# The last two pairs of token tiles: one after the other instead of side by side

## The chip, the cores and the metric

One core of a Trainium2 chip. The time is device microseconds of one execution of the whole program; less is better. The core's engines run side by side and wait for one another through semaphores: TensorE (PE, matmuls; PEld is its weight load) writes to PSUM, VectorE (DVE) and ScalarE (ACT) read PSUM and write SBUF, GpSimd (POOL) works on SBUF, and SyncE (SP) issues most of the transfers.

## The reference

Attention within clusters on 4 batches of 8 heads, 768 positions, 64 dimensions; its output, as 3072 tokens of 512, goes through a gated feed-forward layer:

```python
x = np.ascontiguousarray(attn_out.transpose(0, 2, 1, 3)).reshape(B * S, H * D)
gate = 1.0 / (1.0 + np.exp(-(x @ w_gate)))    # 512 x 1536
val = x @ w_val                               # 512 x 1536
return (gate * val @ w_out).astype(np.float32)  # w_out: 1536 x 512
```

Only the end of the feed-forward layer is touched here.

## The kernel before

**Stages.** The batches go one after the other. Attention of a batch writes transposed tokens `xT`; the feed-forward work of a batch is cut into two blocks of 384 tokens (three tiles of 128), put into a list `queue` of small pieces ("atoms") and taken from there between attention steps by `ffn_run`, which has a budget in ns. When all attention is done, the last block (batch 3, block 1, tiles 3 to 5) is queued with `final=True` and runs to the end with nothing else beside it but `aside` (below).

**Gate and value groups** (`ffn_atoms`). For each of the 12 slices `fc` of the 1536 hidden values, a gate atom does four matmuls of 384 columns into a bank of the PSUM `ring` (L529) and a tanh on ScalarE (L535); a value atom does four more into the next ring bank (L545), and VectorE joins both into slice `fc` of `hT` (L550). The ring has four banks handed out in turn; a bank is written again only when its last reader is done.

**Output products** (`product_out`). From batch 1 on, `hT @ w_out` is done for pairs of token tiles (t1, t2) in a scheme with seven products instead of eight. With the hidden dimension cut into two halves of 6 slices, and the 512 output columns into two of 256, the left side is a 2x2 matrix of blocks (row: t1 or t2; column: hidden half), and so is `w_out` (B11, B12, B21, B22; T1 to T4 are sums of them made once). The sums of the left side are made by VectorE (`Sums.make`, L626 to L632): 1 = both halves of t2, 2 = sum 1 - t1's first half, 3 = t1's first half - t2's first half, 4 = t1's second half - sum 2, written over sum 2. A product of one pair is six matmuls of 256 columns (L713), in this order:

| product | left | adds into | what follows |
|---|---|---|---|
| 1 | t1, first half | x, fresh | ScalarE copies x to C11 |
| 4 | t2, second half | y, fresh | C21 = y + C11 |
| 6 | sum 2 | x, fresh | C12 = x + C11 |
| 5 | sum 1 | y, fresh | C22 = y + C11, then sum 4 |
| 7 | sum 3 | x, on top of 6 | C21 += x, C22 += x, store row t2 |
| 3 | sum 4 | y, on top of 5 | C12 += y |
| 2 | t1, second half | x (last block: a ring bank) | C11 += it, store row t1 |

The additions are `plus` (L658), the copy L662. `x` and `y` are the two banks of the PSUM pool `op`, taken through `out_bank`, which hands the two out in turn. `begin` decides which of them is x:

```python
slot = taken["op"] % 2
u = [out_bank() for _ in range(2)]
x = 0 if slot != taken["last"] else 1
taken["last"] = (slot + x) % 2
```

In block 0 of a batch there is one pair, (0,1): its 14 atoms (half products of three matmuls) go to the list `aside`, and `ffn_run` then takes an atom from `aside` and one from `queue` by turns. In batch 3 they so alternate with the first 14 gate and value atoms of the last block. In block 1 there are two pairs, (3,2) and (4,5) (tile 2 was left over from block 0). They run **side by side**: each product is done for both pairs, in the two halves of one bank, and an addition covers both (512 columns). In the last block the products start after all 12 gate and value groups. Product 2 is there done by `closing` (L727): (3,2) whole, (4,5) in two halves of 128 columns, each into a ring bank of its own, each with its addition and its store.

When the sums are made is in a table: after value group `fc`, these sums of these pairs.

```python
1: [(1, (3, 2))], 5: [(2, (3, 2)), (3, (3, 2))], 6: [(3, (4, 5))],
11: [(1, (4, 5)), (2, (4, 5))],
```

**Stores** (`store`, L502). One transfer on SP's queue for each; in batch 3 it is issued as soon as SP reaches it and its data is ready. SP works strictly in order. Output tiles `ob` are `[128, 2, 512]` floats: row 0 is t1's, row 1 t2's (side by side: one tile for both t1, one for both t2).

Of the kernel before, what the change touches and what calls it, by code (L numbers as in the profile page):

```python
# [8 lines left out]
FP = mybir.dt.float32  # L9
HP = mybir.dt.float16  # L10
# [88 lines left out]
def kernel(  # L99
# [397 lines left out]
    def tok(b, t, f):  # L497
        return HB[b, t // 3][:, HF * f : HF * f + HF, bass.ts(t % 3, 128)]
# [16 lines left out]
    def ffn_atoms(xT, t0, n, b, final=False):  # L515
        blk = t0 // 384
        gv = []
        cost = NDC * max(n, 80) / 2.4 + 3
        pairs = [] if b < PB else [(0, 1)] if blk == 0 else [(3, 2), (4, 5)]
        sm = {x: Sums(b, *x) for x in pairs}  # L520

        def gate(fc, st):
            def f():
                need(("w", fc // WQ, 0), *(("x", b, p, t0 // 128 + c) for p in range(NP) for c in range(n // 128)))
                if fc == 0:
                    HB[b, blk] = htp.tile([128, NFC, 384], HP, name="hT")
                g = bank(512, name="g")
                for dc in range(NDC):
                    PE.matmul(  # L529
                        out=g[:, 0:n], lhsT=wg[fc // WQ][:, dc, fc % WQ, :],  # L530
                        rhs=xT[:, dc, t0 : t0 + n],
                        start=(dc == 0), stop=(dc == NDC - 1),
                    )
                th = thp.tile([128, 384], FP, name="th")
                ACT.activation(th[:, 0:n], g[:, 0:n], AF.Tanh)  # L535
                st.append(th)

            return f

        def val(fc, st):  # L540
            def f():
                need(("w", fc // WQ, 1))
                w = bank(512, name="v")
                for dc in range(NDC):
                    PE.matmul(  # L545
                        out=w[:, 0:n], lhsT=wv[fc // WQ][:, dc, fc % WQ, :],
                        rhs=xT[:, dc, t0 : t0 + n],
                        start=(dc == 0), stop=(dc == NDC - 1),
                    )
                DVE.scalar_tensor_tensor(  # L550
                    HB[b, blk][:, fc, 0:n], st[0][:, 0:n], 1.0, w[:, 0:n], ALU.add, ALU.mult
                )
                for k, x in SUMS_AT[b >= PB, blk].get(fc, []):
                    sm[x].make(k)
                if fc == NFC - 1 and pairs and blk == 0:
                    aside.extend(product_out(b, [sm[(0, 1)]], False))

            return f

        for fc in range(NFC):  # L560
            st = []
            gv.append((cost, gate(fc, st)))
            gv.append((cost, val(fc, st)))
        outs = []
        if b < PB:
            for t in range(n // 128):
                outs += plain_out(b, blk, t)
        elif blk == 1:
            outs = product_out(b, [sm[x] for x in pairs], final)
        return gv + outs  # L570

    def plain_out(b, blk, t):
        OA = SCHED.get(f"oa{b}{384 * blk}", SCHED.get("oa", 4))
# [33 lines left out]
        },  # L607
    }

    class Sums:  # L610


        def __init__(self, b, t1, t2):
            self.b, self.t1, self.t2, self.of = b, t1, t2, {}

        def make(self, i):
            a1 = lambda f: tok(self.b, self.t1, f)
            a2 = lambda f: tok(self.b, self.t2, f)
            if i == 4:
                self.of[4] = self.of[2]  # L620
            else:
                t = sump.tile([128, HF, 128], HP, tag="sum", name="sum")
                self.of[i] = t
            o = self.of[i]
            if i == 1:
                DVE.tensor_tensor(o, a2(0), a2(1), ALU.add)  # L626
            elif i == 2:
                DVE.tensor_tensor(o, self.of[1], a1(0), ALU.subtract)
            elif i == 3:
                DVE.tensor_tensor(o, a1(0), a2(0), ALU.subtract)  # L630
            else:
                DVE.tensor_tensor(o, a1(1), o, ALU.subtract)  # L632

    def product_out(b, sums, final):


        P_ = len(sums)
        st = {}

        def begin():  # L640
            need(*(("wo", i) for i in range(WOP)), *(("wt", i, c) for i in range(4) for c in range(2)))
# [4 lines that stand above are left out]
            taken["pair"] = True  # L646
            for z, t in (("x", u[x]), ("y", u[1 - x])):
                st[z] = t[:, 0 : P_ * HD].rearrange("p (e m) -> p e m", m=HD)
            if P_ == 1:
                ob = osp.tile([128, 2, DM], FP, name="ob")  # L650
                st["o1"], st["o2"] = ob[:, 0:1], ob[:, 1:2]
            else:
                st["o1"] = osp.tile([128, 2, DM], FP, name="ob")
                st["o2"] = osp.tile([128, 2, DM], FP, name="ob")
            for o in ("o1", "o2"):
                st[o, 0], st[o, 1] = st[o][:, :, 0:HD], st[o][:, :, HD:DM]

        plus = lambda dst, a, z: DVE.tensor_tensor(dst, a, z, ALU.add)  # L658
        C11, C12, C21, C22 = ("o1", 0), ("o1", 1), ("o2", 0), ("o2", 1)

        def end1():
            ACT.activation(st[C11], st["x"], AF.Copy)  # L662

        def end4():
            plus(st[C21], st["y"], st[C11])

        def end6():
            plus(st[C12], st["x"], st[C11])

        def end5():  # L670
            plus(st[C22], st["y"], st[C11])
            for m in sums:
                m.make(4)

        def end7():
            plus(st[C21], st["x"], st[C21])
            plus(st[C22], st["x"], st[C22])
            for i, m in enumerate(sums):
                store(st["o2"][:, i], b, m.t2, 1)

        def end3():
            plus(st[C12], st["y"], st[C12])
            if final:
                store(st[C12], b, sums[0].t1, P_, slice(HD, DM))

        def end2():
            plus(st[C11], st["x"], st[C11])
            taken["pair"] = False
            store(st["o1"], b, sums[0].t1, P_)

        steps = [
            ("x", lambda m: tok(b, m.t1, 0), B11, True, end1),
            ("y", lambda m: tok(b, m.t2, 1), T4, True, end4),
            ("x", lambda m: m.of[2], T2, True, end6),
            ("y", lambda m: m.of[1], T1, True, end5),
            ("x", lambda m: m.of[3], T3, False, end7),
            ("y", lambda m: m.of[4], B22, False, end3),
            ("x", lambda m: tok(b, m.t1, 1), B21, True, end2),
        ]
        atoms = []  # L700
        G = SCHED.get("og", 3)

        def atom(k, e, g):
            z, lhs, rhs, start, end = steps[k]

            def f():
                if k + e + g == 0:
                    while aside and P_ > 1:
                        aside.pop(0)[1]()
                    begin()  # L710
                a = lhs(sums[e])
                for c in range(g, g + G):
                    PE.matmul(  # L713
                        out=st[z][:, e], lhsT=a[:, c, :], rhs=rhs[:, c, :],
                        start=start and c + e == 0, stop=c == HF - 1, skip_group_check=True,
                    )
                if g + G == HF and e == P_ - 1:
                    end()

            return f  # L720

        def closing(e, a, z):
            def f():
                o = bank(z - a, name="o_end")
                lhs = tok(b, sums[e].t1, 1)
                for c in range(HF):
                    PE.matmul(  # L727
                        out=o, lhsT=lhs[:, c, :], rhs=B21[:, c, a:z],
                        start=c == 0, stop=c == HF - 1,
                    )  # L730
                m = st["o1"][:, e, a:z]
                plus(m, o, m)
                store(m.unsqueeze(1), b, sums[e].t1, 1, slice(a, z))

            return f

        for k in range(6 if final else 7):
            for e in range(P_):
                for g in range(0, HF, G):
                    atoms.append((G * (HD / 2.4 + 2.5), atom(k, e, g)))  # L740
        if final:
            for e, a, z in ((0, 0, HD), (1, 0, HD // 2), (1, HD // 2, HD)):
                atoms.append((900, closing(e, a, z)))
        return atoms

    queue = []
# [754 lines left out]
```

## Time and profile before

| | us |
|---|---|
| three runs: median (lowest to highest) | 324.35 (324.08 to 324.59) |
| the profiled run | 324.13 |
| its span in the profile | 322.3 |
| busy in the span: TensorE, ScalarE, VectorE, GpSimd | 314.6, 231.3, 226.4, 108.6 |

The span runs from the first to the last recorded instruction; the run's own time is 1.8 us longer. In the profile's lines, a group is given as line, engine, operation, output<-inputs, shape and count; in a timeline, start and length come first. A matmul's recorded length reaches past the start of the next one: matmuls overlap, so their rate is read from starts. The clock is that granted to TensorE, 1.00 being full.

### The profile page before, as it was taken

To read this page: it belongs to the slowest core of one execution; us is meant where nothing else is said; L and a number is where in the kernel's file an instruction comes from. 1 tells how busy PE (TensorE), PEld (TensorE's weight loads), DVE (VectorE), ACT (ScalarE), POOL (GpSimd) and SP (SyncE) were. 2 spreads that over 40 slices of the span, in tenths; PEclk is the share of its full clock that TensorE was granted. 3 is DMA by queue.
4 is the path that set the end of the run, shared out by engine and by line. 5 is a ranking of instruction groups with operands and counts; after the bars stand their busy time and mean duration, and the time that the engine had idled before them with its cause. 6 is when DMAs were issued, how large, how long until landed. Compare 5 with 4: busy or idle time off the path is not lost.

```text
span 322.3 us, 9168 instructions
## 1 busy us (share of the span) xinstructions
PE 314.6 (98%) x3510; PEld 222.1 (69%) x3510; DVE 226.4 (70%) x588; ACT 231.3 (72%) x520; POOL 108.6 (34%) x145
## 2 busy tenths in 40 slices
PE   7999999999999999999999999999999999999995
PEld 5888666766766656666777687666777688566674
DVE  5899656777667997576879588676867356555655
ACT  6688988787898977877767866788777886332220
POOL 5887464154335275433143342523111111000000
PEclk9999999999999999999999999999999999999999
DMA  6999996738988677974694652952503112200103
GB/s 205 379 253 171 259 169 120 205 85 232 248 121 226 112 218 153 229 175 130 116 212 121 202 113 60 288 124 52 111 2 91 39 26 79 77 2 1 67 0 130
DMA packets 77835, 45.15 MB, mean 140 GB/s; under 512 B 56864, under 2 KB 75232, under 8 KB 77792
## 3 DMA queue, kind: packets, MB, share of 16 engines
q1 hardware_dynamic: 73824, 39.73, 48.2%
q0 software_dynamic: 3680, 4.72, 9.0%
q8 instruction: 27, 0.44, 0.6%
q14 instruction: 16, 0.13, 0.1%
q10 hardware_dynamic: 288, 0.13, 0.1%
HBM read 28.34 MB, written 6.29 MB: 107 GB/s over the span
## 4 chain that ended last, share of the span: by engine, by line
PE 91%; DVE 6%; issue 1%; ACT 1%; ACTq 0%; POOL 0%; DVEq 0%
PE g L529 19%; PE v L545 19%; PE sc L803 18%; PE o L713 12%; PE av L826 10%; PE o L583 4%; PE lg L434 2%; PE lg L421 1%; PE t_ps L1052 1%; PE oh_ps L1112 1%; DVE lgs L449 0%; DVE T L1065 0%; DVE vheld L276 0%; PE vs_ps L354 0%; PE o_end L727 0%
## 5 line engine op out<-in xcount | busy, mean ns | idle before, releaser
L808 ACT ACTIVATE es<-sc 128x384 f16<-128x384 f32 x384 | 174.7, 492 | 40.0 <-PE sc L803 30.7
L803 PE MATMUL sc<-T 128*128 128x384 f16 x384 | 117.8, 326 | 1.0 <-DVE lgs L449 0.6
L826 PEld LDWEIGHTS <-es 128*128 128x128 f16 x1152 | 81.4, 98 | 35.3 <-issue 0.2
L826 PE MATMUL av<-va,es 128*128 128x65 f16 x1152 | 97.6, 194 | 0.0
L550 DVE SCALAR_TENSOR_TENSOR hT<-th,v 128x384 f16<-128x384 f32 x96 | 53.1, 553 | 55.8 <-PE av L826 36.6
L529 PE MATMUL g<-xTb,wg 128*128 128x384 f16 x384 | 78.2, 326 | 0.1
L545 PE MATMUL v<-xTb,wv 128*128 128x384 f16 x384 | 78.1, 326 | 0.0
L535 ACT ACTIVATE th<-g 128x384 f32<-128x384 f32 x96 | 47.2, 492 | 32.8 <-PE g L529 13.7
L375 POOL TENSOR_TENSOR xp<-t,rec 128x384 f16<-128x384 f32 (+1 forms) x30 | 21.8, 728 | 100.4 <-DVE rec L372 49.9
L529 PEld LDWEIGHTS <-wg 128*128 128x128 f16 x384 | 37.2, 97 | 19.7 <-issue 0.4
L545 PEld LDWEIGHTS <-wv 128*128 128x128 f16 x384 | 37.4, 98 | 19.0
L803 PEld LDWEIGHTS <-T 128*128 128x128 f16 x384 | 37.1, 97 | 0.7 <-DVE T L1133 0.7
L1369 POOL TENSOR_TENSOR hl<-kraw,hl 128x384 f16<-128x384 f32 x22 | 20.2, 920 | 42.0 <-DVE hl L1368 19.6
L658 DVE TENSOR_TENSOR ob<-o,ob 128x256 f32<-128x256 f32 (+1 forms) x41 | 21.9, 547 | 8.8 <-PE o L713 8.1
L713 PEld LDWEIGHTS <-sum 128*128 128x128 f16 x216 | 20.9, 98 | 5.6 <-DVE sum L632 0.7
L1369 POOL TENSOR_TENSOR hl<-qraw,hl 128x384 f16<-128x384 f32 x22 | 20.7, 940 | 10.0 <-DVE hl L1368 9.7
L713 PE MATMUL o<-wo,hT 128*128 128x256 f16 x150 | 22.5, 272 | 0.0
L370 DVE TENSOR_TENSOR t<-av,sv 128x390 f32<-128x390 f32 (+1 forms) x30 | 14.4, 479 | 8.2 <-PE av L826 7.3
L583 PE MATMUL o<-wo,hT 128*128 128x512 f16 x72 | 19.9, 379 | 0.0
L713 PEld LDWEIGHTS <-hT 128*128 128x128 f16 x150 | 14.6, 97 | 3.7
L449 DVE TENSOR_REDUCE lgs<-lg 128x192 f32<-128x384 f32 x23 | 12.7, 550 | 2.8 <-PE lg L434 2.6
L322 POOL CAST va<-vraw 128x768 f16<-128x768 f32 x15 | 13.0, 868 | 2.6 <-DMA vraw<-in_v_dram 2.6
(143 smaller groups left out, 324.9 us busy)
## 6 DMA issues: line engine op xcount, KB each, us to landing
vraw<-in_v_dram SPq DMA_DIRECT2D x15, 384.0 KB, 4.8
kraw<-in_k_dram SPq DMA_DIRECT2D x14, 384.0 KB, 4.0
out_dram<-ob SPq DMA_DIRECT2D x19, 256.0 KB, 2.3
qraw<-in_q_dram SPq DMA_DIRECT2D x12, 384.0 KB, 4.3
wg<-in_moe_w_gate_dram POOLq DMA_DIRECT2D x2, 768.0 KB, 9.6
wv<-in_moe_w_val_dram POOLq DMA_DIRECT2D x2, 768.0 KB, 10.6
wo<-in_moe_w_out_dram POOLq DMA_DIRECT2D x2, 768.0 KB, 9.3
T<-ohT SPq DMA_DIRECT2D x44, 24.0 KB, 1.9
```

Of the source, the lines that this page charges most:

```text
L375: (eng or POOL).tensor_tensor(x, t[:, 0:nq, 0:64], bcast(rec[:, 0:nq], 64), ALU.mult)
L529: PE.matmul(out=g[:, 0:n], lhsT=wg[fc // WQ][:, dc, fc % WQ, :], rhs=xT[:, dc, t0 : t0 + n], start=(dc == 0), stop=(dc == NDC - 1),)
L535: ACT.activation(th[:, 0:n], g[:, 0:n], AF.Tanh)
L545: PE.matmul(out=w[:, 0:n], lhsT=wv[fc // WQ][:, dc, fc % WQ, :], rhs=xT[:, dc, t0 : t0 + n], start=(dc == 0), stop=(dc == NDC - 1),)
L550: DVE.scalar_tensor_tensor(HB[b, blk][:, fc, 0:n], st[0][:, 0:n], 1.0, w[:, 0:n], ALU.add, ALU.mult)
L583: PE.matmul(out=o, lhsT=HB[b, blk][:, fc, bass.ts(t, 128)], rhs=wo[fc // WON][:, fc % WON, :], start=(fc == 0), stop=(fc == NFC - 1),)
L658: plus = lambda dst, a, z: DVE.tensor_tensor(dst, a, z, ALU.add)
L713: PE.matmul(out=st[z][:, e], lhsT=a[:, c, :], rhs=rhs[:, c, :], start=start and c + e == 0, stop=c == HF - 1, skip_group_check=True,)
L803: PE.matmul(out=sc.rearrange("p (c t) -> p c t", t=128), lhsT=s["k"], rhs=s["q"], start=True, stop=True,)
L808: ACT.activation(es, sc, AF.Exp, scale=SCALE)
L826: PE.matmul(out=av[:, a0 + s["c0"] + i, :], lhsT=s["es"][:, bass.ts(i, 128)], rhs=VA[b, p][:, e, s["j"], :], start=(first and i == 0 and a ...
L1369: POOL.tensor_tensor(hl[:, :, 64:128], r, hl[:, :, 0:64], ALU.subtract)
```

## The change

`product_out` loses its `final` branch. The last block's pairs are done by a new function `closing`: the first four products (1, 4, 6, 5) of (3,2) are cut in halves of three matmuls, and one half goes behind each of the atoms from gate group 7 to value group 10; gate and value group 11 follow. Then, whole: 7 of (3,2); 1 and 4 of (4,5); 3 of (3,2); 6 and 5 of (4,5); 2 of (3,2); 7 and 3 of (4,5); 2 of (4,5) in two halves. Pair (3,2) has the two banks of `op`; pair (4,5) takes four ring banks for its x and y (1 and 4, then 6 and 5), and product 2 takes ring banks as before. An addition covers one pair (256 columns). Stores: after product 7 row t2 (256 KB), after 3 the right half of row t1 (128 KB), after 2 the left half (128 KB, for (4,5) one store after both halves). The sums that need the last slices are made in two parts, slices 0 to 4 of a half after value group 10 and slice 5 after group 11; sum 4 has a tile of its own.

```diff
+        when = SUMS_LAST if final else SUMS_AT[b >= PB, blk]
...
-                for k, x in SUMS_AT[b >= PB, blk].get(fc, []):
-                    sm[x].make(k)
+                for k, x, *c in when.get(fc, []):
+                    sm[x].make(k, *c)
...
-            outs = product_out(b, [sm[x] for x in pairs], final)
+            outs = product_out(b, [sm[x] for x in pairs])
+        if final:
+            return closing(b, gv, sm[(3, 2)], sm[(4, 5)])
         return gv + outs
+
+    def closing(b, gv, ma, mb):
...
+            rhs = {1: B11, 2: B21, 3: B22, 4: T4, 5: T1, 6: T2, 7: T3}
...
+            def product(k, g=0, n=HF):
+                def f():
+                    z = {1: "a", 4: "d", 6: "x", 7: "x", 5: "y", 3: "y"}[k]
+                    if g == 0 and k in (1, 4, 6, 5):
+                        if k == 1:
+                            st["ob"] = osp.tile([128, 2, DM], FP, name="ob")
+                        st[z] = bk(z)
+                    o = st[z][:, 0:HD]
+                    mm(o, k, g, n, k not in (7, 3))
+                    if g + n < HF:
+                        return
+                    if k == 1:
+                        ACT.activation(C(0, 0), o, AF.Copy)
+                    elif k == 4:
+                        plus(C(1, 0), o, C(0, 0))
+                    elif k == 6:
+                        plus(C(0, 1), o, C(0, 0))
+                    elif k == 5:
+                        plus(C(1, 1), o, C(0, 0))
+                    elif k == 7:
+                        plus(C(1, 0), o, C(1, 0))
+                        plus(C(1, 1), o, C(1, 1))
+                        store(st["ob"][:, 1:2], b, m.t2, 1)
+                    else:
+                        plus(C(0, 1), o, C(0, 1))
+                        store(st["ob"][:, 0:1, HD:DM], b, m.t1, 1, slice(HD, DM))
...
+            def last(parts):
+                def f():
+                    for a, z in parts:
+                        o = bank(z - a, name="o_end")
+                        mm(o, 2, 0, HF, True, a, z)
+                        plus(st["ob"][:, 0, a:z], o, st["ob"][:, 0, a:z])
+                    store(st["ob"][:, 0:1, 0:HD], b, m.t1, 1, slice(0, HD))
...
+        def bank_a(z):
+            if z in "ad":
+                need(*(("wo", i) for i in range(WOP)), *(("wt", i, c) for i in range(4) for c in range(2)))
+                two[z] = out_bank()
+            return two[{"x": "a", "y": "d"}.get(z, z)]
+
+        pa, la = pair(ma, bank_a)
+        pb, lb = pair(mb, lambda z: bank(512, name="o_end"))
+        early = [pa(k, g, HF // 2) for k in (1, 4, 6, 5) for g in (0, HF // 2)]
...
+        early[0] = drained(early[0])
+        atoms = gv[:14]
+        for i, x in enumerate(gv[14:]):
+            atoms.append(x)
+            if i < len(early):
+                atoms.append((0.0, early[i]))
+        for f in (
+            pa(7), pb(1), pb(4), pa(3), pb(6), pb(5), la([(0, HD)]), pb(7), pb(3),
+            lb([(0, HD // 2), (HD // 2, HD)]),
+        ):
+            atoms.append((0.0, f))
+        return atoms
...
+    SUMS_LAST = {
+        1: [(1, (3, 2))], 5: [(2, (3, 2)), (3, (3, 2))], 6: [(3, (4, 5))],
+        10: [(4, (3, 2), 0, 5), (1, (4, 5), 0, 5), (2, (4, 5), 0, 5), (4, (4, 5), 0, 5)],
+        11: [(4, (3, 2), 5, 6), (1, (4, 5), 5, 6), (2, (4, 5), 5, 6), (4, (4, 5), 5, 6)],
+    }
```

More of the change, by code (lines that the diff above doesn't have):

```diff
@@ L552, in f @@
                 )
-                for k, x in SUMS_AT[b >= PB, blk].get(fc, []):
-                    sm[x].make(k)
+                for k, x, *c in when.get(fc, []):
+                    sm[x].make(k, *c)
                 if fc == NFC - 1 and pairs and blk == 0:
-                    aside.extend(product_out(b, [sm[(0, 1)]], False))
+                    aside.extend(product_out(b, [sm[(0, 1)]]))
             return f
@@ L568, in ffn_atoms, with pair, mm, drained @@
         elif blk == 1:
-            outs = product_out(b, [sm[x] for x in pairs], final)
+            outs = product_out(b, [sm[x] for x in pairs])
+        if final:
+            return closing(b, gv, sm[(3, 2)], sm[(4, 5)])
         return gv + outs
+    def closing(b, gv, ma, mb):
+        ac, order = [], []
+        plus = lambda dst, a, z: DVE.tensor_tensor(dst, a, z, ALU.add)
+        def pair(m, bk):
+            st = {}
+            lhs = {
+                1: lambda: tok(b, m.t1, 0), 2: lambda: tok(b, m.t1, 1), 4: lambda: tok(b, m.t2, 1),
+                6: lambda: m.of[2], 5: lambda: m.of[1], 7: lambda: m.of[3], 3: lambda: m.of[4],
+            }
+            rhs = {1: B11, 2: B21, 3: B22, 4: T4, 5: T1, 6: T2, 7: T3}
+            C = lambda i, j: st["ob"][:, i, HD * j : HD * j + HD]
+            def mm(o, k, g, n, start, a=0, z=HD):
+                w = lhs[k]()
+                for c in range(g, g + n):
+                    PE.matmul(
+                        out=o, lhsT=w[:, c, :], rhs=rhs[k][:, c, a:z],
+                        start=start and c == 0, stop=c == HF - 1, skip_group_check=True,
+                    )
+            def product(k, g=0, n=HF):
[24 more added lines that the diff above has]
+                        store(st["ob"][:, 0:1, HD:DM], b, m.t1, 1, slice(HD, DM))
+                return f
+            def last(parts):
[5 more added lines that the diff above has]
+                    store(st["ob"][:, 0:1, 0:HD], b, m.t1, 1, slice(0, HD))
+                return f
+            return product, last
+        two = {}
+        def bank_a(z):
[6 more added lines that the diff above has]
+        early = [pa(k, g, HF // 2) for k in (1, 4, 6, 5) for g in (0, HF // 2)]
+        def drained(f):
+            def g():
+                while aside:
+                    aside.pop(0)[1]()
+                f()
+            return g
+        early[0] = drained(early[0])
[10 more added lines that the diff above has]
+        return atoms
@@ L608 @@
     }
+    SUMS_LAST = {
[3 rows of a table added]
+    }
     class Sums:
@@ L614, in __init__, with make @@
             self.b, self.t1, self.t2, self.of = b, t1, t2, {}
[L616 to L624, printed above, removed]
+        def make(self, i, c0=0, c1=HF):
+            c = slice(c0, c1)
+            a1 = lambda f: tok(self.b, self.t1, f)[:, c]
+            a2 = lambda f: tok(self.b, self.t2, f)[:, c]
+            if c0 == 0:
+                if i == 4 and c1 == HF:
+                    self.of[4] = self.of[2]
+                elif i == 4:
+                    self.of[4] = tp.tile([128, 12, 128], HP, tag="T", name="T")[:, 0:HF]
+                else:
+                    self.of[i] = sump.tile([128, HF, 128], HP, tag="sum", name="sum")
+            o = self.of[i][:, c]
             if i == 1:
@@ L627, in make @@
             elif i == 2:
-                DVE.tensor_tensor(o, self.of[1], a1(0), ALU.subtract)
+                DVE.tensor_tensor(o, self.of[1][:, c], a1(0), ALU.subtract)
             elif i == 3:
@@ L631, in make, with product_out @@
             else:
-                DVE.tensor_tensor(o, a1(1), o, ALU.subtract)
-    def product_out(b, sums, final):
+                DVE.tensor_tensor(o, a1(1), self.of[2][:, c], ALU.subtract)
+    def product_out(b, sums):
         P_ = len(sums)
@@ L682, in end3 @@
             plus(st[C12], st["y"], st[C12])
-            if final:
-                store(st[C12], b, sums[0].t1, P_, slice(HD, DM))
         def end2():
@@ L720, in atom @@
             return f
[L722 to L737, printed above, removed]
+        for k in range(7):
             for e in range(P_):
@@ L740, in product_out @@
                     atoms.append((G * (HD / 2.4 + 2.5), atom(k, e, g)))
-        if final:
-            for e, a, z in ((0, 0, HD), (1, 0, HD // 2), (1, HD // 2, HD)):
-                atoms.append((900, closing(e, a, z)))
         return atoms
```

## The prediction

> **What bounds the kernel now.** I read the page first: busy time, the clock, the chain that ended last.
>
> ```profile
> span 322.3 us, 9168 instructions
> PE 314.6 (98%) x3510; PEld 222.1 (69%) x3510; DVE 226.4 (70%) x588; ACT 231.3 (72%) x520; POOL 108.6 (34%) x145
> PEclk9999999999999999999999999999999999999999
> PE 91%; DVE 6%; issue 1%; ACT 1%; ACTq 0%; POOL 0%; DVEq 0%
> ```
>
> TensorE is busy 98% of the span at full granted clock, and the chain is 91% TensorE. The program's matmuls stay the same in number and shape, so the change can move time only in two ways: TensorE gaps after the point where the two programs part, and what follows the last matmul. That point is gate group 7 of the last block: both programs issue the same up to there. So next I read the chain in order of time, and the windows of the last 20 us.
>
> ```profile
> 302.23 0.33 PE o L713 x3
> 302.56 0.65 PE g L529 x4
> 309.06 7.98 PE o L713 x72
> 317.04 1.34 PE o_end L727 x18
> 318.38 0.02 issue
> 318.40 0.29 DVE ob L658
> 302.40:309.06 6.66, 6.66 (x44) 4.06 (x42) 3.52 (x7) 2.46 (x5) 0.00 (x0) 1.00 0.11 42
> 309.06:318.40 9.34, 9.30 (x91) 8.05 (x88) 7.07 (x13) 0.60 (x1) 0.00 (x0) 1.00 0.04 15
> 318.40:321.40 3.00, 0.00 (x0) 0.00 (x0) 0.29 (x1) 0.00 (x0) 0.00 (x0) 1.00 0.86 302
> ```
>
> (In the windows, after the length: busy us of PE, PEld, DVE, ACT, POOL, then clock, DMA share, GB/s.) The prices of TensorE are here: a group of four 384-column matmuls takes 0.65 us, three 256-column ones 0.33, so a product of one pair (six) 0.65; the 18 closing matmuls take 1.34, of which 6 are 256 wide (0.65), so each half of the last product costs 0.345. TensorE has no gap worth naming, and it ends at 318.40. The last 3.9 us are stores. Their issues, and the time to landing:
>
> ```profile
> 317.19 0.33 SPq L502 DMA_DIRECT2D out_dram<-ob  x1
> 317.57 0.42 SPq L502 DMA_DIRECT2D out_dram<-ob  x1
> 318.09 0.40 SPq L502 DMA_DIRECT2D out_dram<-ob  x1
> 318.60 0.44 SPq L502 DMA_DIRECT2D out_dram<-ob  x1
> 319.63 0.40 SPq L502 DMA_DIRECT2D out_dram<-ob  x1
> out_dram<-ob SPq DMA_DIRECT2D x5, 256.0 KB, 2.0
> out_dram<-ob SPq DMA_DIRECT2D x1, 128.0 KB, 2.4
> out_dram<-ob SPq DMA_DIRECT2D x2, 64.0 KB, 1.8
> ```
>
> Six stores, 1 MB, start between 317.19 and 319.63 (the fifth falls between the last two), about 0.51 us apart, because SP issues them one by one. The last addition on VectorE ends at 318.40+0.29 = 318.69, yet its store is issued at 319.63: **0.94 us of queueing**. It lands at 319.63+1.8 = 321.43; the other 0.9 us to the span's end is closing work that stays.
>
> **The change part by part.** *Stores spread: a gain at the end.* The six stores keep their 1 MB (256, 128, 128 KB for pair (3,2), the same for (4,5)), but pair (3,2)'s are issued while the products of (4,5) run, so behind the last matmul stand only 256, 128 and 128 KB, each started when its addition is done. The last is one 128 KB store where there were two of 64. The trace has one of 128 KB, in a crowd (2.4 us); from the 2.0 us of the 256 KB stores, less 128 KB at the 302 GB/s of the window (0.4), an estimate without a crowd is 1.6. Bounds 1.6 to 2.4; I take 1.7, near the low end, since the store ahead carries only 128 KB and starts 0.5 us before.
> The Trainium skill, "DMA: Bandwidth & Descriptors", section "Anatomy of one DMA", gives a fixed 2.0 us and the bytes at 436 GB/s (for the path that software drives, which SP's is not); by that the 128 KB would take about 2.3 us, and the sum below would be 0.6 us later. The 64 KB stores, which landed in 1.8, speak against it.
>
> *Bank of the first product: a new TensorE wait.* Pair (3,2)'s first product now starts after gate group 7 and takes the next of the two output banks (`out_bank`). Following the bookkeeping of `begin` through the program: the pair (0,1), finished just before, took both banks and chose the first as its "x"; so the next one handed out is that x, whose last reader is the addition after the pair's seventh product. The old `begin` picks the other bank ("x = 0 if slot != last"); the new code doesn't look. The rows:
>
> ```profile
> 302.07 0.49 PE L713 MATMUL o<-wo,hT 128*128 128x256 f16 x3
> 302.34 0.55 DVE L550 SCALAR_TENSOR_TENSOR hT<-th,v 128x384 f16<-128x384 f32 x1
> 302.40 0.81 PE L529 MATMUL g<-xTb,wg 128*128 128x384 f16 x4
> 302.81 0.55 DVE L630 TENSOR_TENSOR sum<-hT 128x768 f16<-128x768 f16 x1
> 303.05 0.81 PE L545 MATMUL v<-xTb,wv 128*128 128x384 f16 x4
> 303.28 0.42 DVE L658 TENSOR_TENSOR ob<-o,ob 128x256 f32<-128x256 f32 x1
> 314.14 1.47 PE L713 MATMUL o<-vheld,sum 128*128 128x256 f16 x12
> 314.95 1.01 DVE L632 TENSOR_TENSOR sum<-hT,sum 128x768 f16<-128x768 f16 x2
> 315.55 1.49 PE L713 MATMUL o<-wo,sum 128*128 128x256 f16 x12
> 315.55 1.21 PEld L713 LDWEIGHTS <-sum 128*128 128x128 f16 x12 [0.22 <-DVE sum L632]
> ```
>
> The seventh product's last matmuls start at 302.07, but VectorE first does hT 6 and a sum, so the addition runs from 303.28 to 303.70. TensorE reaches the first product at 303.05. From VectorE's end to TensorE's start is 0.05 (the first L632 ends at 314.95+0.55 = 315.50, the load starts at 315.55). So TensorE waits until 303.75: **+0.70 us**. Value group 7 and all behind it stand queued in order, and ScalarE and VectorE wait for those. Bounds: 0 if the bank is not shared, 0.70 if it is; I take 0.70.
>
> *Early products among the groups.* They move 24 matmuls, no more: nothing on TensorE (groups and products already alternate at 0.65 and 0.33 before 302). Their additions and the ScalarE copy lie in VectorE's and ScalarE's idle time (3.5 and 2.5 us busy of 6.7).
>
> *Sums split over groups 10 and 11.* This loads VectorE at the worst place. Prices:
>
> ```profile
> L626 DVE TENSOR_TENSOR sum<-hT 128x768 f16<-128x768 f16 x1 | 0.6, 559 | 0.0
> L658 DVE TENSOR_TENSOR ob<-o,ob 128x512 f32<-128x512 f32 x6 | 4.0, 687 | 2.0 <-PE o L713 2.0
> L658 DVE TENSOR_TENSOR ob<-o_end,ob 128x128 f32<-128x128 f32 x2 | 0.6, 288 | 0.0
> L550 DVE SCALAR_TENSOR_TENSOR hT<-th,v 128x384 f16<-128x384 f32 x2 | 1.1, 554 | 1.5 <-PE v L545 1.5
> 308.25 0.81 PE L545 MATMUL v<-xTb,wv 128*128 128x384 f16 x4
> 309.17 0.55 DVE L550 SCALAR_TENSOR_TENSOR hT<-th,v 128x384 f16<-128x384 f32 x1 [0.75 <-PE v L545]
> 310.35 0.56 DVE L628 TENSOR_TENSOR sum<-sum,hT 128x768 f16<-128x768 f16 x1
> ```
>
> From 687 (512 columns) and 288 (128): 1.04 ns a column and 155 ns fixed. For f16, 559-155 over 768 is 0.53 ns, so five chunks (640) cost 0.49 and one chunk 0.22. Bounds: five chunks 0.47 to 0.56 (by proportion; as a whole sum), one chunk 0.09 to 0.56; a chunk by the nearest row (128 columns) would be 0.29. Independent VectorE instructions overlap by 0.08 (302.34+0.55 against 302.81), one that needs its predecessor starts about 0.03 after it. hT starts 0.27 after its group's issue ends (308.25+0.65 to 309.17).
> With the bank wait, value group 10 is issued by 303.75+7x0.65+7x0.33 = 310.6, and hT 10 runs 310.85 to 311.4. Behind it in VectorE's order stand four sums (to 313.4), the fourth product's addition (to 313.7) and only then hT 11: 313.63 to 314.18, though group 11 ended at 312.2. Of TensorE's work the fourth product (k=4) of (4,5) needs hT 11, in its sixth matmul, due at 313.52+0.54 = 314.06: it starts at 314.23, **+0.17 us**. Then four one-chunk sums and the additions in a row; by this sum VectorE works without a break to 317.2 and has caught up there with 0.3 us to spare.
>
> *Ring banks at the end.* Pair (4,5) uses the ring of four. The last half-product takes the bank that its seventh product's second addition reads until 318.61; due at 318.60, it starts at 318.66: **+0.06**. What goes: today's wait for L632, 0.22 on the loads, 0.10 on TensorE (315.55 instead of 314.14+12x0.109 = 315.45): **-0.10**.
>
> *Sum.* Last matmul: +0.70+0.17+0.06-0.10 = +0.83, issue ends near 319.0. The last addition starts 0.2 later as now and ends at 319.5. SP: 318.63, 319.14, 319.65 at 0.51 apart, so the last store is issued at 319.65 (now 319.63), and lands at 319.65+1.7 = 321.35 (now 321.43). **Net -0.1 us.** The profiled run took 324.13 against a span of 322.3, so 324.05 for it; the median of the three runs, 324.35, is 0.22 above the profiled one: **324.3 us**.
>
> **The rivals.** (1) *No bank wait*: if the next bank is free, or VectorE's addition came before the sum, 0.70 is gone, all else stays: last store at 318.95, 323.6 us. For: the trace has no buffer numbers. Against: two banks, both just used, handed out in turn.
> (2) *VectorE becomes the bound*, on the slower side: if one-chunk sums cost 0.40 and five-chunk ones 0.56 (no cheaper for being short), hT 11 is later by 4x0.07 = 0.28, and the four short sums add 0.7 to a run that has 0.3 to spare. It decides from some 0.35 us of VectorE work beyond my sum; at these prices the last store is issued at about 320.5, 0.9 late: 325.2 us. For: four dependent instructions, twice, where three stand now. Against: the fixed part above is small.
> (3) *The change doesn't do what it says*: the stores are still a crowd (512 KB within a microsecond of issues) and the last lands in 2.4 us, as the 128 KB one now: +0.7, 325.0. For: the DMA engines are 86% busy in the last 3 us now. Against: at 302 GB/s 256 KB take 0.85 us, and the two issues behind it come 0.5 and 1.0 later.
> (4) *The clock falls*: TensorE now pauses between groups; if a gate group, a value group and their two pieces (0.65+0.65+0.33+0.33 = 1.96 us) run at half clock, they take 1.96 longer: 326.3. Against: granted clock 1.00 in every window above.
> The Trainium skill, "TensorE: Matmul & The Clock Gate", section "A second HAM failure mode: psum-queue depth-cycling", says that short idles between groups that cycle through banks make the clock swing to half. No window here shows it.
>
> **How the numbers follow.** My case 0.60 (its own range 323.9 to 324.8: the landing by 0.3, sums by 0.2), (1) 0.18, (2) 0.12, (3) 0.07, (4) 0.03. About 0.2% (0.65 us) is what a measurement of this kernel can tell from no change, so faster is below 323.7 and slower above 325.0. Faster: most of (1) and a little of my case, 0.19; slower: (2), (4) and half of (3), 0.17; between, 0.64. The range of 8 in 10 takes in (1) and reaches into (2): 323.5 to 325.2.
>
> **What would show it.** A TensorE gap of 0.7 us before the first early product, released by L658's addition: its absence makes (1) right. hT 11 starting over 1 us after its group ends, and a short wait in the fourth product of (4,5). The last store issued near 319.65, at most 0.2 us after its addition's end, landing in 1.7. I am wrong if the last matmul ends before 318.6 or after 319.5, or if another TensorE wait appears.

## The result, and the profile after

The changed kernel takes 323.4 us (median of 12 runs, 323.0 to 324.03), the kernel before 324.3 (12 runs beside it). The ratio is 0.9969, with a 95% interval from 0.9958 to 0.998: **faster by 0.3%** (0.9 us between the medians, 1.0 by the ratio). The forecast was 324.3 and no change; the time lies 0.1 below the range, and near the first rival, "no bank wait", at 323.6.

The profiles' starts wander: the last gate group 7, up to which all programs of this study are the same, starts at 302.40 in the profile of before and 302.82 in that after, and between 302.12 and 303.14 in the experiments. So I compare stretches that begin there. First, pieces of the changed kernel's chain of waits in order of time (start, length), two windows at its end (columns as in the prediction), and its last stores on SP:

```profile
302.98 0.65 PE g L530 x4
314.90 3.96 PE o_end L594 x42
318.86 0.02 issue
318.89 0.29 DVE ob L580
318.88:321.00 2.12, 0.00 (x0) 0.00 (x0) 0.29 (x1) 0.00 (x0) 0.00 (x0) 1.00 0.68 247
319.50:320.50 1.00, 0.00 (x0) 0.00 (x0) 0.00 (x0) 0.00 (x0) 0.00 (x0) 1.00 1.06 383
318.35 0.33 SPq L502 DMA_DIRECT2D out_dram<-ob  x1
318.77 0.38 SPq L502 DMA_DIRECT2D out_dram<-ob  x1
319.25 0.40 SPq L502 DMA_DIRECT2D out_dram<-ob  x1
out_dram<-ob SPq DMA_DIRECT2D x1, 256.0 KB, 2.1
out_dram<-ob SPq DMA_DIRECT2D x2, 128.0 KB, 1.9
```

(The last two rows: the three stores issued after 318, with their median time to landing.) TensorE ends at 318.86, that is 16.04 us behind gate group 7; before it was 318.38-302.40 = 15.98. **TensorE's side hardly moved.** The last store is issued at 319.25, 16.43 behind gate group 7, where it was 319.63-302.40 = 17.23: **0.80 earlier**. From there to the span's end it is 321.9-319.25 = 2.65 (before 322.3-319.63 = 2.67). The crowd of stores around the last matmul is now three stores and 512 KB in place of six and 1 MB. From gate group 7 to the span's end it is 19.08 us in place of 19.90, 0.82 less, and all of that is in the stores. (The spans are given to a tenth of a us, so such differences are good to about 0.1.) The crowd is smaller, not gone: the window from 319.50 to 320.50 has all 16 DMA engines busy, at 383 GB/s.

The point that decided, in the timeline of the changed kernel (start, length, engine, line; the addition that reads pair (0,1)'s x last is L768 now):

```profile
302.82 0.81 PE L530 MATMUL g<-xTb,wg 128*128 128x384 f16 x4
303.47 0.49 PE L594 MATMUL o<-wo,hT 128*128 128x256 f16 x3
303.70 0.42 DVE L768 TENSOR_TENSOR ob<-o,ob 128x256 f32<-128x256 f32 x1
303.80 0.81 PE L546 MATMUL v<-xTb,wv 128*128 128x384 f16 x4
```

The early product starts at 303.47, right behind the gate group, while the addition has yet to start. So it writes a bank that this addition does not read; the 0.70 us of waiting isn't there.

VectorE at groups 10 and 11, and the one wait of TensorE's that is left:

```profile
310.58 0.55 DVE L551 SCALAR_TENSOR_TENSOR hT<-th,v 128x384 f16<-128x384 f32 x1 [1.07 <-PE v L546]
311.17 0.49 DVE L742 TENSOR_TENSOR T<-hT,sum 128x640 f16<-128x640 f16 x1
312.62 0.49 DVE L742 TENSOR_TENSOR T<-hT,sum 128x640 f16<-128x640 f16 x1
313.03 0.42 DVE L580 TENSOR_TENSOR ob<-o,ob 128x256 f32<-128x256 f32 x1
313.37 0.54 DVE L551 SCALAR_TENSOR_TENSOR hT<-th,v 128x384 f16<-128x384 f32 x1
313.94 0.22 DVE L742 TENSOR_TENSOR T<-hT,sum 128x128 f16<-128x128 f16 x1
311.29 0.81 PE L546 MATMUL v<-xTb,wv 128*128 128x384 f16 x4
312.59 1.66 PE L594 MATMUL o_end<-wo,hT 128*128 128x256 f16 x12
313.96 0.10 PEld L594 LDWEIGHTS <-hT 128*128 128x128 f16 x1 [0.29 <-DVE hT L551]
314.09 0.82 PE L594 MATMUL o<-wo,T 128*128 128x256 f16 x6
318.02 0.83 PE L594 MATMUL o_end<-wo,hT 128*128 128x128 f16 x12
```

Value group 11's issue ends at 311.94 and its hT could start 0.27 later, at 312.21; it starts at 313.37, behind four sums and an addition. Products 1 and 4 of (4,5) then need 12 matmuls, 12x0.109 = 1.31 us, but the next one starts at 314.09 instead of 313.90: 0.19 lost. The last 12 half-wide matmuls run without a gap.

### The profile page after: what moved, and what is told of

It reads as the page before. It is cut to its first block, busy times and chain, and to the rows that moved or that the text cites. A ratio compares the mean times of both kernels' runs of the same rounds, so it can differ in the third digit from the quotient of the medians.

```text
span 321.9 us, 9182 instructions
## 1 busy us (share of the span) xinstructions
PE 314.6 (98%) x3510; PEld 222.3 (69%) x3510; DVE 227.1 (71%) x598; ACT 231.3 (72%) x521; POOL 108.6 (34%) x145
## 4 chain that ended last, share of the span: by engine, by line
PE 87%; DVE 6%; issue 3%; POOL 1%; DMA 1%; ACT 1%; ACTq 0%; POOLq 0%; DVEq 0%
PE g L530 19%; PE v L546 19%; PE sc L893 17%; PE av L916 10%; PE o L821 7%; PE o L684 4%; PE lg L434 2%; PE o_end L594 2%; PE o L594 1%; PE lg L421 1%; PE t_ps L1142 1%; DMA xTb<-xp 1%; PE oh_ps L1202 1%; DVE hT L551 1%; POOL xp L375 1%
## 5 line engine op out<-in xcount | busy, mean ns | idle before, releaser
L768 DVE TENSOR_TENSOR ob<-o,ob 128x256 f32<-128x256 f32 (+1 forms) x35 | 17.9, 523 | 6.7 <-PE o L821 6.0
L821 PE MATMUL o<-wo,hT 128*128 128x256 f16 x126 | 19.7, 272 | 0.0
L821 PEld LDWEIGHTS <-sum 128*128 128x128 f16 x168 | 16.3, 98 | 4.8 <-DVE sum L742 0.5
L821 PEld LDWEIGHTS <-hT 128*128 128x128 f16 x126 | 12.2, 97 | 3.4
```

The lines of the kernel that those rows point to most:

```text
L821: PE.matmul(out=st[z][:, e], lhsT=a[:, c, :], rhs=rhs[:, c, :], start=start and c + e == 0, stop=c == HF - 1, skip_group_check=True,)
```

## The experiments

All stretches in one table, from each kernel's own profile; "start" is where gate group 7 starts, TensorE's end is the end of its last piece in the chain, the ratio that to the kernel before.

| kernel | start | to TensorE's end | to the last store's issue | from there to the span's end | ratio (95%) |
|---|---|---|---|---|---|
| before | 302.40 | 15.98 | 17.23 | 2.67 | 1 |
| changed | 302.82 | 16.04 | 16.43 | 2.65 | 0.9969 (0.9958 to 0.998) |
| e1_bank | 302.38 | 16.74 | 17.13 | 2.69 | 1.0 (0.9987 to 1.0013) |
| e2_held | 303.14 | 16.05 | 17.93 | 2.63 | 1.0034 (1.0022 to 1.0046) |
| e3_two_queues | 302.30 | 15.98 | 16.33 | 3.97 | 1.0012 (1.0 to 1.0024) |
| e4_no_early | 302.59 | 17.21 | 17.60 | 2.71 | 1.0016 (1.0005 to 1.0027) |
| e5_sums_at_9 | 302.14 | 15.86 | 16.25 | 2.71 | 0.9956 (0.9939 to 0.9973) |
| e6_no_early_sums_at_9 | 302.29 | 16.32 | 16.72 | 2.69 | 0.9982 (0.9971 to 0.9992) |
| e7_one_last_store | 302.12 | 15.98 | 16.75 | 3.13 | 1.0001 (0.9991 to 1.001) |
| e8_row_earlier | 302.20 | 15.86 | 16.24 | 2.56 | 0.996 (0.9946 to 0.9975) |
| e9_take_order | 302.35 | 16.05 | 16.44 | 2.71 | 0.9966 (0.9946 to 0.9986) |

My theory after the result: the first product's bank is free, and the gain is what stands behind the last matmul. Rivals: the bank was shared but its wait costs nothing; the early products or the order on TensorE bring the gain.

**e1_bank.** The first product led to the bank that I had feared:

```diff
-                two[z] = out_bank()
+                if z == "a":
+                    two["d"], two["a"] = out_bank(), out_bank()
+                    PE.matmul(
+                        out=two["d"][:, 0:128], lhsT=warm[:, 0:128], rhs=warm[:, 0:128],
+                        start=True, stop=True,
+                    )
```

> The changed kernel, but pair (3,2)'s first product is led to the bank that the addition after pair (0,1)'s seventh product reads last (a throw-away matmul of 128 columns, about 0.06 us, touches the other bank first). If the changed kernel's first product has the other, free bank, as its profile without a TensorE gap suggests, this brings the wait that the prediction had priced: a gap of 0.6 to 0.75 us before the first early product, about 324.1 us and a ratio near 0.999 to the kernel before. If the bank was shared already, or such a wait costs nothing (it is hidden), time and gaps stay as in the changed kernel, about 323.4.

It took 324.08 us, ratio 1.0. In its timeline TensorE, behind the throw-away matmul, waits for VectorE (the last addition is L773 here):

```profile
303.03 0.22 PE L647 MATMUL o<-wo 128*128 128x128 f16 x1
303.26 0.42 DVE L773 TENSOR_TENSOR ob<-o,ob 128x256 f32<-128x256 f32 x1
303.73 0.49 PE L594 MATMUL o<-wo,hT 128*128 128x256 f16 x3 [0.48 <-DVE ob L773]
```

The product starts at 303.73, 0.70 later than the end of gate group 7's issue at 303.03, and every later point moves by the same 0.70 (16.43 to 17.13 in the table). So the price was right and the wait is not hidden; with it the change would have brought nothing, as forecast. Only, the changed kernel's first product goes to the other bank.

**e9_take_order.** The two banks taken in the opposite order, written in the same:

```diff
-                two[z] = out_bank()
+                if z == "a":
+                    two["d"], two["a"] = out_bank(), out_bank()
```

> The changed kernel with the two output banks of (3,2) taken in the opposite order (the one for product 4 first, then the one for product 1), but written in the same order as before. If the order in which they are taken decides which bank is which, as the prediction assumed, product 1 now gets the other bank, and since it met no wait in the changed kernel it meets one here: a TensorE gap of 0.6 to 0.7 us behind gate group 7, ratio near 0.999. If the first write decides, nothing changes: no gap, 16.4 us from gate group 7 to the last store's issue, ratio 0.997.

323.23 us, ratio 0.9966, and no gap:

```profile
302.35 0.81 PE L530 MATMUL g<-xTb,wg 128*128 128x384 f16 x4
303.00 0.49 PE L594 MATMUL o<-wo,hT 128*128 128x256 f16 x3
```

The order of taking decides nothing. With e1_bank, which differs from it by one throw-away matmul, it shows that the first write decides: the tile that is written first gets the bank whose last reader comes first (y's), the second gets x's. That the order of release decides which bank the first write gets is argued from these cases, not tested further.

**e2_held.** The stores of (3,2) held back behind the first of (4,5):

```diff
+        held_ = []
+
+        def late(m, *a):
+            if m is ma:
+                held_.append(a)
+                return
+            store(*a)
+            while held_:
+                store(*held_.pop(0))
...
-                        store(st["ob"][:, 1:2], b, m.t2, 1)
+                        late(m, st["ob"][:, 1:2], b, m.t2, 1)
```

(and so for the other two stores of a pair).

> The changed kernel with the three stores of pair (3,2) put behind the first store of pair (4,5), nothing else moved. Theory (the gain is the spread of the stores on SP's queue): six stores start at 318.4 after the same start, some 0.5 us apart, so the last is issued 1.4 to 1.5 us later than in the changed kernel and lands in 1.7 to 1.8: about 324.9, slower than the kernel before by 0.5. Rival (the gain comes from the order of the products or from TensorE): 323.4 as in the changed kernel.

325.16 us, ratio 1.0034; TensorE's stretch is unchanged at 16.05, the last issue 1.50 later than in the changed kernel. The gain and more is lost by the stores' places alone, so the rival of TensorE's order falls. The loss is larger than the 0.5 us expected against the kernel before: 0.7 to 1.5 us by the interval, 0.66 in the trace (20.56 against 19.90 from gate group 7 to the span's end). First and fourth of the six issues, and the DMA engines in the windows behind:

```profile
318.67 0.33 SPq L502 DMA_DIRECT2D out_dram<-ob  x1
320.01 0.46 SPq L502 DMA_DIRECT2D out_dram<-ob  x1
319.40:320.40 1.00, 0.00 (x0) 0.00 (x0) 0.10 (x1) 0.00 (x0) 0.00 (x0) 1.00 0.93 356
320.40:321.40 1.00, 0.00 (x0) 0.00 (x0) 0.00 (x0) 0.00 (x0) 0.00 (x0) 1.00 1.05 383
```

The engines are full as well as SP's queue is, so this run doesn't say which of the two binds. The next two do.

**e3_two_queues.** The kernel before, with its six last stores by turns on SP's and ScalarE's queues (`store` gets a parameter `eng` for the queue):

```diff
...
-                store(st["o2"][:, i], b, m.t2, 1)
+                store(st["o2"][:, i], b, m.t2, 1, eng=ACT if final and i else None)
...
-                store(m.unsqueeze(1), b, sums[e].t1, 1, slice(a, z))
+                store(m.unsqueeze(1), b, sums[e].t1, 1, slice(a, z), eng=None if e and not a else ACT)
```

> The kernel before with its last six stores taken by turns from SP's and ScalarE's queues (three each), nothing else moved. If the 0.94 us between the last addition and its store were the issues one by one on SP alone, the last store starts within 0.1 to 0.2 us of its addition and the time falls by 0.8, to about 323.5. If the transfers themselves are the limit (1 MB in some 2.9 us behind 318.0), the last landing moves by 0.2 at most: 324.1.

324.54 us, ratio 1.0012: no gain at all. The last issues on SP and on ScalarE, three windows, and three of the groups of stores with their time to landing:

```profile
318.32 0.39 SPq L502 DMA_DIRECT2D out_dram<-ob  x1
318.63 0.64 ACTq L502 DMA_DIRECT2D out_dram<-ob  x1
318.00:319.00 1.00, 0.27 (x5) 0.09 (x2) 0.55 (x3) 0.00 (x0) 0.00 (x0) 1.00 1.04 395
319.00:320.00 1.00, 0.00 (x0) 0.00 (x0) 0.00 (x0) 0.00 (x0) 0.00 (x0) 1.00 1.06 381
321.00:321.20 0.20, 0.00 (x0) 0.00 (x0) 0.00 (x0) 0.00 (x0) 0.00 (x0) 0.61 0.07 20
out_dram<-ob SPq DMA_DIRECT2D x2, 256.0 KB, 2.9
out_dram<-ob SPq DMA_DIRECT2D x1, 64.0 KB, 3.2
out_dram<-ob ACTq DMA_DIRECT2D x1, 64.0 KB, 3.1
```

The issues are done 0.9 earlier (16.33 against 17.23), and each store takes 3 us to land instead of 2: the 16 DMA engines have 1.04 and 1.06 of work in these windows, at 380 to 395 GB/s. The kernel before has its engines just as full:

```profile
318.00:319.00 1.00, 0.36 (x7) 0.19 (x4) 0.65 (x3) 0.00 (x0) 0.00 (x0) 1.00 0.99 379
319.00:320.00 1.00, 0.00 (x0) 0.00 (x0) 0.00 (x0) 0.00 (x0) 0.00 (x0) 1.00 1.07 390
321.00:321.20 0.20, 0.00 (x0) 0.00 (x0) 0.00 (x0) 0.00 (x0) 0.00 (x0) 1.00 0.00 0
```

It is the megabyte that takes its time, not the queue. The end is even 0.4 later than before, and the windows at 321.00 show where: with two queues a few last packets still move, 0.07 of 16 engines, about the work of a single one, until about 321.3 (19.0 behind gate group 7); in the kernel before the bytes are done by 320.9 (18.5). Why so few engines were left with work is not shown.

**e7_one_last_store.** The kernel before with its last two 64 KB stores joined:

```diff
-                store(m.unsqueeze(1), b, sums[e].t1, 1, slice(a, z))
+                if e == 0:
+                    store(m.unsqueeze(1), b, sums[e].t1, 1, slice(a, z))
+                elif a:
+                    store(st["o1"][:, e : e + 1, 0:HD], b, sums[e].t1, 1, slice(0, HD))
```

> The kernel before, with the last two 64 KB stores joined to one of 128 KB (five stores, 1 KB rows in the place of 512 bytes). If one issue after the other on SP sets the end, the last issue is 0.5 us earlier (319.1) and the time falls by 0.4 to 0.5, ratio 0.9985. If the DMA engines' bytes set it, as e3_two_queues suggests, the time stays within 0.15 us, but for what the wider rows bring (at most 0.1): ratio 0.9995 to 1.0.

324.0 us, ratio 1.0001. The last issue and the two windows behind the last matmul:

```profile
318.87 0.41 SPq L502 DMA_DIRECT2D out_dram<-ob  x1
318.00:319.00 1.00, 0.09 (x2) 0.00 (x0) 0.37 (x2) 0.00 (x0) 0.00 (x0) 1.00 1.05 401
319.00:320.00 1.00, 0.00 (x0) 0.00 (x0) 0.00 (x0) 0.00 (x0) 0.00 (x0) 1.00 1.07 376
```

The last issue is 0.48 earlier (16.75), and from it to the end it takes 0.46 longer (3.13). One issue less and wider rows bring nothing while the bytes are the same: the megabyte is what bound the end (1 MB at some 380 GB/s is 2.8 us).

**e4_no_early.** The four first products of (3,2) behind all groups:

```diff
-        early = [pa(k, g, HF // 2) for k in (1, 4, 6, 5) for g in (0, HF // 2)]
+        early = [pa(k) for k in (1, 4, 6, 5)]
...
+        atoms = list(gv)
         for f in (
-            pa(7), pb(1), pb(4), pa(3), pb(6), pb(5), la([(0, HD)]), pb(7), pb(3),
+            *early, pa(7), pb(1), pb(4), pa(3), pb(6), pb(5), la([(0, HD)]), pb(7), pb(3),
```

> The changed kernel with pair (3,2)'s first four products behind all gate and value groups instead of among groups 7 to 10; pairs still one after the other, stores as in the changed kernel. Theory (only the stores at the end matter): TensorE has the same work in the end, the last stores are the same, so 323.4 within 0.2; the wait for hT 11 in the fourth product of (4,5) is gone (-0.2), small waits for the copy and addition between the first products of (3,2) may come (+0.1 to +0.3). Rival (the early products are what pays): the gain is lost, 324.2 or more.

324.73 us, ratio 1.0016: my expectation failed, slower than the changed kernel by the intervals. The wait is one of TensorE's, before product 5; VectorE runs the sums until then:

```profile
310.40 0.82 PE L594 MATMUL o<-qheld,sum 128*128 128x256 f16 x6
312.40 0.81 PE L594 MATMUL o<-kheld,sum 128*128 128x256 f16 x6 [1.19 <-DVE ob L580]
310.51 0.55 DVE L551 SCALAR_TENSOR_TENSOR hT<-th,v 128x384 f16<-128x384 f32 x1
311.92 0.76 DVE L580 TENSOR_TENSOR ob<-o,ob 128x256 f32<-128x256 f32 x2
```

Product 5 overwrites the bank that the addition after product 4 reads; this addition stands on VectorE behind hT 11 and eight sums and starts at 311.92. The early products keep it away from that pile: with the sums split in this way they are needed.

**e6_no_early_sums_at_9.** The same with the sums made at groups 9 and 11:

```diff
-        10: [(4, (3, 2), 0, 5), (1, (4, 5), 0, 5), (2, (4, 5), 0, 5), (4, (4, 5), 0, 5)],
-        11: [(4, (3, 2), 5, 6), (1, (4, 5), 5, 6), (2, (4, 5), 5, 6), (4, (4, 5), 5, 6)],
+        9: [(4, (3, 2), 0, 4), (1, (4, 5), 0, 4), (2, (4, 5), 0, 4), (4, (4, 5), 0, 4)],
+        11: [(4, (3, 2), 4, 6), (1, (4, 5), 4, 6), (2, (4, 5), 4, 6), (4, (4, 5), 4, 6)],
```

> The products of (3,2) again behind all groups (as in e4_no_early), with the sums split at groups 9 and 11. In e4_no_early TensorE stood 1.19 us before product 5, for an addition that came behind the sums on VectorE. If VectorE's backlog is the cause, the wait shrinks to 0.2 to 0.5 us, and most of the loss goes: 323.6 to 323.9, ratio 0.998 to 0.999. If it is the two banks themselves (a bank can't be written again in the time that one product takes), the wait stays near 1.2: 324.6.

323.5 us, ratio 0.9982. The wait for the same bank is down to 0.30:

```profile
311.22 0.82 PE L594 MATMUL o<-kheld,sum 128*128 128x256 f16 x6 [0.30 <-DVE ob L580]
```

So VectorE's backlog made most of the 1.19, not the turn of the two banks. No run tests the sums of the kernel before with the pairs one after the other.

**e5_sums_at_9.** The changed kernel, early products and all, with that table of sums.

> The changed kernel with the first part of the split sums made after value group 9 (slices 0 to 3 of a half) and the second after group 11 (slices 4 and 5). If hT 11 is late because four sums stand before it on VectorE, it now starts within 0.5 us of its group's end, the wait of TensorE in the fourth product of (4,5) (0.19 us in the changed kernel) is gone, and the stretch from gate group 7 to the last store's issue shrinks from 16.43 us by about 0.2, to 16.2: ratio near 0.9963. If VectorE's total work is what binds the end, nothing is gained.

322.86 us, ratio 0.9956. hT 11 starts at 311.53 and the wait in the fourth product of (4,5) is gone:

```profile
310.61 0.81 PE L546 MATMUL v<-xTb,wv 128*128 128x384 f16 x4
311.53 0.55 DVE L551 SCALAR_TENSOR_TENSOR hT<-th,v 128x384 f16<-128x384 f32 x1 [0.18 <-PE v L546]
311.92 1.47 PE L594 MATMUL o_end<-wo,hT 128*128 128x256 f16 x12
```

The 12 matmuls record 1.47 instead of 1.66, and the stretch to the last issue is 0.18 shorter.

**e8_row_earlier.** e5_sums_at_9 with another order of the last products:

```diff
-            pa(7), pb(1), pb(4), pa(3), pb(6), pb(5), la([(0, HD)]), pb(7), pb(3),
+            pa(7), pb(1), pb(4), pb(6), pb(5), pa(3), pb(7), la([(0, HD)]), pb(3),
```

> e5_sums_at_9 with the last products in the order 6 and 5 of (4,5), 3 of (3,2), 7 of (4,5), 2 of (3,2), 3 and 2 of (4,5): the 256 KB store leaves 0.65 us earlier, and the last three stores carry 384 KB in place of 512. If in the changed kernel the last store no longer waits for bytes ahead of it (it lands in 1.7), this brings at most 0.1 over e5_sums_at_9: ratio 0.996 to 0.9963. If the crowd still holds it, 0.2 to 0.3 more.

322.76 us, ratio 0.996: as e5_sums_at_9 within the intervals. In the profile the last issue is the same (16.24) and the end 0.15 nearer to it (2.56 against 2.71), hardly more than the rounding. The last store lands in 1.7, where in the changed kernel it took 1.9:

```profile
out_dram<-ob SPq DMA_DIRECT2D x1, 128.0 KB, 1.7
```

In e5, with the order of the changed kernel, it is 1.8. So the crowd that is left costs the last store 0.1 to 0.2 us. Both e5 and e8 have lower ratios than the changed kernel, with intervals that overlap its own; in the stretch to the span's end they are shorter than its 19.08 us by 0.12 (16.25+2.71 = 18.96) and 0.28 (16.24+2.56 = 18.80). Both beat the kernel before by their intervals.

## Why the prediction was wrong, step by step

- **What bounds the kernel**: right. TensorE's work is the same before and after, and the time moved in what stands behind its end.
- **Stores spread**: right in size. The last store was to go from 17.23 to 16.55 behind gate group 7 without the bank wait; it went to 16.43. Wrong in its cause: "0.94 us of queueing" on SP was there, but taking it away brought nothing. With fewer issues (e7) or two queues (e3) the end doesn't come earlier, because 1 MB at some 380 GB/s takes 2.8 us. Rival (3) looked for such a crowd in the changed kernel, at 0.7 us; there it costs 0.1 to 0.2 (the last store landed in 1.9, not 1.7; e8), and it was the kernel before that had the large one.
- **Bank of the first product**: this step failed. It said "so the next one handed out is that x" from the order of taking in the code. The order of taking decides nothing (e9); the first write does (e1 against e9), and the first product got the bank that was released earlier: it starts at 303.47, before the addition it was to wait for (303.70). So the +0.70, put into the sum in full, was 0. The price was exact (e1), only not due: 0.70 of the 0.9 us by which the forecast was off is this one term, 324.3-0.70 = 323.6, and the rest (0.2) is within the other terms and the runs' scatter. The prediction's own sign of being wrong came too: the last matmul ended 15.98+0.06 behind gate group 7, which is 318.44 on the time axis of the profile before and ahead of the 318.6 that it had named.
- **Early products**: "nothing on TensorE" holds. What they are worth the prediction didn't say: put behind the groups they cost 1.17 us with the changed sums (e4: 17.60 against 16.43), 0.47 with the sums at 9 and 11 (e6 against e5: 16.72 against 16.25).
- **Sums split**: right. 0.49 and 0.22 measured as priced, hT 11 started 1.43 after its group's issue ended (313.37 against 311.94; forecast 313.63 against 312.2), TensorE's wait 0.19 (0.17 forecast); e5 removes it. Only VectorE caught up 0.4 later than by the sum (at 317.33, 14.51 behind gate group 7, where 317.2 less the bank wait is 14.10), and no further wait of TensorE came of it.
- **Ring banks**: 0.06 forecast, none seen. The wait for L632 that was to go, -0.10, did go: without the wait for hT 11 TensorE ends 15.86 behind gate group 7 (e5), 0.12 before the 15.98 of the kernel before.
- **Sums of the prediction**: two don't come out of their own terms. Rival (2)'s 0.28+0.7 with 0.3 to spare is 0.7 late, not 0.9; and the chances for slower, 0.12, 0.03 and half of 0.07, add up to 0.185, not 0.17. Neither bears on the forecast of 324.3.
- **The clock**: granted 1.00 in all windows shown that hold matmuls, so rival (4) didn't come. In e4 TensorE stood 1.19 us between two products and went on at full rate (six matmuls in 0.82 before and 0.81 after the wait), the granted clock 1.00 in the stretch behind it:

```profile
312.40:314.00 1.60, 1.60 (x15) 1.44 (x15) 0.79 (x3) 0.00 (x0) 0.00 (x0) 1.00 0.00 0
```

The Trainium skill, "TensorE: Matmul & The Clock Gate", section "A second HAM failure mode: psum-queue depth-cycling", has frequent short idles between matmul groups make the clock swing. No run here has such frequent idles, so none shows it; the single idle of 1.19 us left the clock where it was.

## What to carry to other kernels

Which physical buffer a tile gets isn't read from the order in which the code takes it; before a wait on it goes into a sum with certainty, look for its condition in an existing trace, or give the two cases the odds of a coin. For a tail of stores, add up the bytes that are issued around the last matmul before blaming the queue: joining two stores is a cheap test that tells the two apart. And on an engine that works in order, put long work that is needed late behind the instruction that the bound engine waits for, or early enough to be done before it.

## What was not expected of the hardware

Stores on two queues at once landed after 2.9 to 3.2 us where the same six on one queue took 1.8 to 2.4, at much the same 379 to 395 GB/s; the end came 0.4 us later (20.30 against 19.90 from gate group 7). The last bytes there came later too, about 19.0 against 18.5, and the last of them at the pace of about one engine of the 16. What leaves so little at the end to so few engines stays open.
